# The tanh of a feed-forward block, moved one attention cycle later, with ScalarE in the program's own order

## The chip, the cores and the metric

The kernel runs on one core of a Trainium2 chip. The metric is the device time of one execution in microseconds (us); lower is better. Before the change three runs gave 1499.8, 1505.9 and 1506.9 us, a median of 1505.9 us. A core has five engines with a queue each: TensorE (PE, matrix products), VectorE (DVE), ScalarE (ACT, here exp and tanh), GpSimd (POOL) and SyncE (SP, which here only issues DMAs). Each works through its own list of instructions, and instructions wait for one another through semaphores.

## The reference

One sequence of 2048 tokens of width 512, float32:

```
h  = x + softmax(q k^T / 4) v @ wo       q = LN(x) @ wq (32 heads of 16), one k and one v for all heads
h2 = h + (gelu(LN(h) @ w_gate) * (LN(h) @ w_up)) @ w_down      w_gate, w_up: 512 x 1792
gelu(g) = 0.5 g (1 + tanh(0.798 (g + 0.0447 g^3)))
```

The two halves are an attention block and a gated feed-forward network (FFN). Every float32 product is made of three products of split halves (high and low parts), so most tensors come in pairs such as `gh`/`gl` or `x2h`/`x2l`.

## The kernel before

The sequence is cut in four blocks of 512 queries. Within a block the attention runs over 8 groups of 4 heads, and in a group over 16 chunks of 128 keys. The unit of the attention is a *score*: two matmuls into one PSUM tile `s` of 128 x 1024 (line 283) and one exp of it on ACT into `p` (line 287). Two scores make one chunk, and each chunk then needs its products with V, `weigh` (line 291), which accumulate in the PSUM tile `acc`. After a group `evacuate` copies `acc` out (`oT`, line 300), sends it through DRAM, and after every second group DVE takes four reciprocals (line 321), multiplies and splits the result into `o_hi` and `o_lo`.

PE is shared. While the attention of block b+1 runs, the FFN of block b (with the output projection before it) is woven in, as the Python generator `dense`. The main loop (after line 660) goes in *cycles*: each has 5 or 6 scores, between them a fixed number of FFN matmuls (`shares`, such as 0, 5, 4, 3, 0), and at its end the products with V of the chunks whose exps are old enough (`finish`). Six cycles make a group. Only two `s` tiles exist in this stage, so the third score of a cycle can't start before the first exp of the cycle is done, and during the products with V there is no score for ACT to work on. The FFN of the last block has no attention to be woven into; it is the tail, from about 1355 us on.

In the FFN, `up(f)` (f from 0 to 13, columns of 128) makes the products `pg` and `pu` in two halves, in two successive cycles (`duo`, line 412). Between the halves a one-column copy on DVE (`mark`, line 420) stands as a wait: the second half swaps the array's halves and starts only behind it. When the second half is through, `up` emits on DVE `g` (a copy of `pg`, line 518), `g*g` (520) and one fused step (521) that leave tanh's argument in `ga`; on ACT the tanh (524); and on DVE again two steps on `ga` (525, 526; the latter reads `pu`) and the split into `gh` and `gl` (lines 104, 105). `down` multiplies `gh`/`gl` with w_down for the four f of one run and adds the product to `h` (546); it is emitted one or two `up`s after the run has ended. PSUM holds three one-bank tiles for all FFN products of the main stage (`width = 3`).

What sets the order of the work: an engine named in `tc.manual_schedule` issues its instructions as the Python code emits them. For the others the framework's planner makes the order when the program is built: it plays the program through with estimated durations, and an engine takes what is ready first, the earlier emitted of two that are both ready. Before the change PE and POOL are manual all through, ACT and DVE in the prologue (`prologue` within `with order`), SP in the first stage (up to about 355 us). So in the main stage ACT's order of exps and tanhs, DVE's order and the order of the DMAs on SP are the planner's. What the order says is then kept on the chip: an instruction that waits holds up all behind it on its engine.

At the start, after `prologue`, `first_q` issues three DMAs on ACT's queue (lines 267 and 271) that wait for the bound `m`; and `rest`, emitted after it, has ACT copy the last two blocks of keys out of PSUM (`leave_k`, lines 841 and 843), which POOL (849), PE (857) and DVE (862, 863) then work on. The first scores need the PSUM banks of this stage.

Of the kernel before, what the change touches and what calls it, by code (L numbers as in the profile page):

```python
# [13 lines left out]
AF = mybir.ActivationFunctionType  # L14
ALU = mybir.AluOpType
# [6 lines left out]
GELU_A = 0.044715  # L22
GELU_C = 0.7978845608028654
# [13 lines left out]
def kernel(  # L37
# [12 lines left out]
    nc = tc.nc  # L50
# [49 lines left out]
    def split(eng_hi, hi, lo, src, eng_lo=None):  # L100
        if eng_hi is nc.scalar:
            nc.scalar.activation(hi, src, AF.Copy)
        else:
            eng_hi.tensor_copy(hi, src)  # L104
        (eng_lo or nc.vector).tensor_tensor(lo, src, hi.bitcast(F32), op=ALU.subtract)  # L105
# [19 lines left out]

    def attend(first):
        with ExitStack() as outer:
            with tc.manual_schedule(engines={mybir.EngineType.PE, mybir.EngineType.Pool}):
                run(outer, first)


    def run(outer, first):
# [3 lines left out]
        def set_banks(name):  # L136
            nonlocal ps
            banks.close()
            ps = banks.enter_context(tc.tile_pool(name=name, bufs=1, space=PSUM))
# [92 lines left out]
        if first:  # L232
            set_banks("ps_pro")
            width = 8
            order = tc.manual_schedule(
                engines={mybir.EngineType.Activation, mybir.EngineType.DVE}
            )
            with order:
                rest = prologue(
                    psum1, xT, wq_hi, wq_lo, sel, k2m, project_q(0, nc.scalar),  # L240
                    advance, eb
                )
# [46 lines left out]
        def weigh(acc, p, kc):  # L289
            for j in range(4):  # L290
                nc.tensor.matmul(  # L291
                    acc[32 * j : 32 * j + 32, :], v_sb[:, kc, :], p[:, j, :],
                    start=(kc == 0), stop=(kc == KC - 1), skip_group_check=True,
                )
# [3 lines left out]
        def evacuate(b, g, acc):  # L298
            oT = sb.tile([P, T], F32, tag="oT", bufs=2, name=f"oT_{b}_{g}")
            nc.vector.tensor_copy(oT, acc)  # L300
            nc.sync.dma_start(acc_d[:, g % 4, :], oT)
            c, k = divmod(g, 2)
            if k == 0:
                pair[0] = sb.tile([P, 2, T], F32, tag="oc", bufs=2, name=f"oc_{b}_{c}")
            oc = pair[0]
            view = acc_d[:, g % 4, :].rearrange("(j s e) t -> j e s t", s=2, e=DH)
            for j in range(4):
                r0 = 64 * k + DH * j
                nc.sync.dma_start(oc[r0 : r0 + DH, :, :], view[j])
            if k == 0:  # L310
                return
            if c == 0:
                o_blk[b] = [
                    sb.tile([P, DC, T], F32R, tag=f"o_{w}", bufs=1, name=f"o_{w}_{b}")
                    for w in ("hi", "lo")
                ]
            hi, lo = o_blk[b]

            for t in range(TB):
                sl = slice(t * P, (t + 1) * P)  # L320
                nc.vector.reciprocal(oc[:, 1, sl], oc[:, 1, sl])  # L321
            nc.vector.tensor_tensor(oc[:, 0, :], oc[:, 0, :], oc[:, 1, :], op=ALU.mult)
            split(nc.vector, hi[:, c, :], lo[:, c, :], oc[:, 0, :])
# [110 lines left out]
        def dense(b, tail=False):  # L434
# [71 lines left out]
            def up(f, gh, gl):  # L506
                hi, lo = w1.pop(f)
                terms = [
                    [
                        (wt[:, k, c, :], xt[:, c, :])  # L510
                        for c in range(DC)
                        for wt, xt in ((hi, xT_hi), (hi, xT_lo), (lo, xT_hi))
                    ]
                    for k in range(2)
                ]
                pg, pu = yield from product([f"pg_{b}_{f}", f"pu_{b}_{f}"], terms)
                g = db.tile([P, T], F32, tag="g", bufs=2, name=f"g_{b}_{f}")
                nc.vector.tensor_copy(g, pg)  # L518
                a = db.tile([P, T], F32, tag="ga", bufs=2, name=f"ga_{b}_{f}")
                nc.vector.tensor_tensor(a, g, g, op=ALU.mult)  # L520
                nc.vector.scalar_tensor_tensor(  # L521
                    a, a, 1.0 / GELU_A, g, op0=ALU.add, op1=ALU.mult
                )
                nc.scalar.activation(a, a, AF.Tanh, scale=GELU_A * GELU_C)  # L524
                nc.vector.scalar_tensor_tensor(a, a, 1.0, g, op0=ALU.add, op1=ALU.mult)  # L525
                nc.vector.tensor_tensor(a, a, pu, op=ALU.mult)
                split(nc.vector, gh[:, f % 2, :], gl[:, f % 2, :], a)
                yield CUT

            def down(fs, gs, last):  # L530
# [54 lines left out]
        def finish(n):  # L585
            for _ in range(min(n, len(pend))):
                pb, pg, pkc, pp, pacc, _ = pend.pop(0)
                weigh(pacc, pp, pkc)
                if pkc == KC - 1:
                    evacuate(pb, pg, pacc)  # L590

        def drain():
            nonlocal work
            for _ in work or ():
                pass
            work = None
# [3 lines left out]
        def score(n):  # L600

            nonlocal acc
            i, u = divmod(n, 2)
            b, r = divmod(i, PER)
            g, kc = divmod(r, KC)
            if u == 0:
                if kc == 0:
                    cur["qg"] = qgs.pop((b, g))
                    acc = pss.tile([P, T], F32, tag="acc", bufs=1, name=f"acc_{b}_{g}")
                if kc == 2 and b * NG + g + 1 < NB * NG:  # L610
                    key = divmod(b * NG + g + 1, NG)
                    qgs[key] = load_q(*key)
                cur["p"] = sb.tile([P, 4, T], F32, tag="p", bufs=PB, name=f"p_{i}")
            scores(i, cur["p"], cur["qg"], kc, u)
            if u == 1:
                pend.append((b, g, kc, cur["p"], acc, n))
# [56 lines left out]
        for c in range(LEAD[0], (NB - 1) * NG * len(SIZES)):  # L673
            b, cb = divmod(c, NG * len(SIZES))
            cg = cb % len(SIZES)
            size, kind = SIZES[cg], None
            if b > 0 and cb == LEAD[b]:
                assert work is None
                work, todo = dense(b), list(kinds)
            if work is not None:  # L680
                kind = todo.pop(0)
            if kind == "long":
                shares = LAST if cg == len(SIZES) - 1 else LONG[size]
            elif kind == "short":
                shares = SHORT[size]
            else:
                shares = PLAIN[size]
            due, said = 0, None
            for share in shares:
                score(n)  # L690
                n += 1
                if kind in (None, "gap"):
                    finish(sum(e[5] < n - 1 for e in pend))
                due += share
                while due > 0:
                    said = next(work)
                    if said > 0:
                        due -= 1
                    elif said == CUT:
                        break  # L700

            while work is not None and kind is not None and said not in (CUT, GAP):
                said = next(work)
                assert said < 0, said
            if work is not None and not todo:
                assert next(work, None) is None
                work = None
            finish(sum(e[5] < n - 1 for e in pend) if cg < len(SIZES) - 1 else len(pend))
        drain()
        banks.close()  # L710
# [234 lines left out]
    def exact_maxima():  # L945
        with ExitStack() as gen:
            sb = gen.enter_context(tc.tile_pool(name="gen", bufs=1))
            ps = gen.enter_context(tc.tile_pool(name="gen_ps", bufs=1, space=PSUM))
            with tc.For_i(0, H, 1) as h:
# [18 lines left out]
                for k in range(2):  # L968
# [4 lines left out]
                    )  # L973

    attend(True)

    safe = nc.values_load(flag[0:1, 0:1], min_val=0, max_val=1)
    with tc.If(safe == 0):
        exact_maxima()
        attend(False)  # L980
# [32 lines left out]
```

## Time and profile before

| what | value |
|---|---|
| median of three runs | 1505.9 us (1499.8 to 1506.9) |
| profiled execution, its own time | 1510.7 us |
| its span, first to last instruction | 1508.9 us |
| PE busy | 1428.4 us, 95% |
| ACT busy | 1040.2 us, 69% |
| DVE busy | 530.1 us, 35% |
| main stage (attention with the FFN woven in) | about 355 to 1355 us |
| tail | about 1355 to 1508.9 us |

How to read it: a row of groups has line, engine, operation, tiles and count, then busy time and mean duration in ns, then the engine's idle time ahead of the group and what ended most of it. A row of the timeline has start and duration in us, and in brackets the idle time before it and what released it. The chain that ended last, followed back from the end, runs over PE for 58% of the span. PE's ends are modelled, so that 95% busy still leaves room for waits between its instructions.

### The profile page before, as it was taken

The numbers are of one execution on the slowest core, as the hardware profiler recorded it, in microseconds if no ns is written. First come the engines' busy times: TensorE is split into PE (matmuls) and PEld (weight loads), VectorE is DVE, ScalarE is ACT, GpSimd is POOL, SyncE is SP. The second block draws the span as 40 slices with busy tenths as digits, with TensorE's granted clock in tenths as the row PEclk, the third lists the DMA queues.
The fourth block names the chain that finished last, engine by engine and source line by source line (L and its number), as shares of the span: only waits on it lengthen the run. The fifth ranks groups of instructions, "written<-read, shape, count | busy, mean of one in ns | idle before, by whom it ended". The sixth has DMA issues, their size and how long they took to land.

```text
span 1508.9 us, 24762 instructions
## 1 busy us (share of the span) xinstructions
PE 1428.4 (95%) x10412; PEld 756.3 (50%) x10412; DVE 530.1 (35%) x915; ACT 1040.2 (69%) x1139; POOL 161.7 (11%) x211
## 2 busy tenths in 40 slices
PE   6899999889999999999999999999999999997998
PEld 4533333224445455455455555554455555555886
DVE  7412221203342431423342332423352332425665
ACT  6499999787777777776677777777677777770000
POOL 5424445430000000000000000000000000000000
PEclk9899999989999999999999999999999999999999
DMA  4425666764122323213222422232232323232552
GB/s 159 150 78 189 224 221 212 224 205 137 56 85 78 137 81 109 94 66 129 67 98 66 137 82 107 97 99 95 68 109 78 113 82 129 72 105 74 194 193 86
DMA packets 76109, 180.53 MB, mean 120 GB/s; under 512 B 8506, under 2 KB 22842, under 8 KB 68790
## 3 DMA queue, kind: packets, MB, share of 16 engines
q1 hardware_dynamic: 75870, 178.81, 35.5%
q8 instruction: 83, 1.36, 0.4%
q14 instruction: 36, 0.29, 0.1%
q10 hardware_dynamic: 120, 0.07, 0.0%
HBM read 131.13 MB, written 47.71 MB: 119 GB/s over the span
## 4 chain that ended last, share of the span: by engine, by line
PE 58%; ACT 13%; DVE 8%; DMA 8%; issue 6%; POOL 5%; SPq 2%; DVEq 0%; POOLq 0%; ACTq 0%
PE acc L291 22%; ACT p L287 12%; PE s L283 11%; PE pu L412 5%; PE pd L412 4%; DMA w_1r<-in_B_w_up_dram 3%; PE pg L429 3%; PE pg L412 3%; PE pd L429 3%; PE pu L429 3%; DVE oc L321 2%; DMA acc_d<-oT 2%; PE pp L412 1%; POOL w_1b L105 1%; PE pq L170 1%
## 5 line engine op out<-in xcount | busy, mean ns | idle before, releaser
L287 ACT ACTIVATE p<-s 128x1024 f32<-128x1024 f32 x1024 | 970.7, 1031 | 261.5 <-PE s L283 260.6
L291 PE MATMUL acc<-p,v_sb 128*32 128x512 f32 x4096 | 496.9, 604 | 2.0 <-DVE oT L300 2.0
L283 PE MATMUL s<-qg,kaug 50*128 50x512 f32 x1984 | 394.1, 436 | 35.3 <-ACT p L287 31.1
L283 PEld LDWEIGHTS s<-qg,kaug 50*128 50x128 f32 x1984 | 172.1, 185 | 320.9 <-ACT p L287 207.6
L291 PEld LDWEIGHTS acc<-p,v_sb 128*32 128x32 f32 x4096 | 112.9, 110 | 252.1 <-issue 243.3
L412 PE MATMUL pu<-x2h,w 64*128 64x512 f32 x672 | 233.6, 394 | 2.4 <-DVE mark_pu L420 0.9
L412 PE MATMUL pg<-x2h,w 64*128 64x512 f32 x672 | 233.5, 394 | 0.8 <-DVE x2h L104 0.8
L412 PEld LDWEIGHTS pu<-x2h,w 64*128 64x128 f32 x672 | 125.1, 186 | 17.8 <-DVE mark_pu L420 3.6
L412 PE MATMUL pg<-x2l,w 64*128 64x512 f32 x336 | 132.1, 393 | 0.1
L412 PE MATMUL pu<-x2l,w 64*128 64x512 f32 x336 | 132.0, 393 | 0.0
L412 PEld LDWEIGHTS pg<-x2h,w 64*128 64x128 f32 x672 | 125.1, 186 | 12.9 <-DVE x2h L104 2.0
L524 ACT ACTIVATE ga<-ga 128x512 f32<-128x512 f32 x56 | 35.3, 631 | 135.6 <-DVE ga L521 135.6
L518 DVE COPY g<-pg 128x512 f32<-128x512 f32 x56 | 38.7, 691 | 232.7 <-PE pg L412 224.5
L113 POOL TENSOR_SCALAR rstd<-mv 128x1 f32<-128x1 f32 x16 | 3.5, 219 | 1041.4 <-DVE mv L111 1041.4
L412 PE MATMUL pd<-w,gh 64*128 64x512 f32 x672 | 105.4, 391 | 0.3 <-DVE mark_pd L420 0.3
L546 DVE TENSOR_TENSOR h<-h,pd 128x512 f32<-128x512 f32 x64 | 41.9, 684 | 138.3 <-PE pd L412 117.3
L321 DVE RECIPROCAL oc<-oc 128x128 f32<-128x128 f32 x64 | 54.1, 907 | 55.9 <-DMA oc<-acc_d 53.9
L412 PEld LDWEIGHTS pd<-w,gh 64*128 64x128 f32 x672 | 63.4, 185 | 15.5 <-issue 0.8
L412 PEld LDWEIGHTS pg<-x2l,w 64*128 64x128 f32 x336 | 62.6, 186 | 8.4 <-DVE x2l L105 1.1
L412 PE MATMUL pd<-w,gl 64*128 64x512 f32 x336 | 66.4, 392 | 0.0
L412 PEld LDWEIGHTS pu<-x2l,w 64*128 64x128 f32 x336 | 62.6, 186 | 6.8
L525 DVE SCALAR_TENSOR_TENSOR ga<-ga,g 128x512 f32<-128x512 f32 x56 | 38.8, 692 | 39.1 <-ACT ga L524 39.1
(176 smaller groups left out, 1219.6 us busy)
## 6 DMA issues: line engine op xcount, KB each, us to landing
w<-w_d SPq DMA_DIRECT2D x84, 1024.0 KB
qg<-q_d SPq DMA_DIRECT2D x62, 200.0 KB
q_d<-qh SPq DMA_DIRECT2D x32, 256.0 KB
acc_d<-oT SPq DMA_DIRECT2D x32, 256.0 KB
oc<-acc_d SPq DMA_DIRECT2D x128, 64.0 KB
w_d<-w_0b SPq DMA_DIRECT2D x14, 512.0 KB
w_d<-w_1b SPq DMA_DIRECT2D x14, 512.0 KB
x<-in_A_x_dram SPq DMA_DIRECT2D x16, 256.0 KB
```

The source lines that it names most:

```text
L105: (eng_lo or nc.vector).tensor_tensor(lo, src, hi.bitcast(F32), op=ALU.subtract)
L170: nc.tensor.matmul(pq, wt[:, d, c * P : (c + 1) * P], xt[:, d, :], start=(n == 0), stop=(n == 3 * DC - 1),)
L283: nc.tensor.matmul(s[:, a, :], kaug[rows, kc * P : (kc + 1) * P], qg[rows, u, :], start=True, stop=True,)
L287: nc.scalar.activation(p[:, 2 * u : 2 * u + 2, :], s, AF.Exp, scale=SCALE)
L291: nc.tensor.matmul(acc[32 * j : 32 * j + 32, :], v_sb[:, kc, :], p[:, j, :], start=(kc == 0), stop=(kc == KC - 1), skip_group_check=True,)
L321: nc.vector.reciprocal(oc[:, 1, sl], oc[:, 1, sl])
L412: nc.tensor.matmul(banks[k], lhsT[rows], rhs[rows], start=(turn == 0 and i == 0), stop=(turn == 1 and i == n - 1), skip_group_check=True,)
L429: nc.tensor.matmul(bank, lhsT, rhs, start=(i == 0), stop=(i == len(ts) - 1))
L518: nc.vector.tensor_copy(g, pg)
L524: nc.scalar.activation(a, a, AF.Tanh, scale=GELU_A * GELU_C)
L525: nc.vector.scalar_tensor_tensor(a, a, 1.0, g, op0=ALU.add, op1=ALU.mult)
L546: nc.vector.tensor_tensor(hs[t], hs[t], pd, op=ALU.add)
```

## The change

ACT is added to the manual engines for the whole of `attend`, so its order is that in which the code emits (the separate mention in the prologue goes, as it is implied). In `up`, the tanh and the four DVE steps behind it (two on `ga`, the split into `gh` and `gl`) are no longer emitted at once but put into a function, `gate`, on a list `gates`. The main loop takes the list at the start of a cycle, and emits what was on it near the end of that cycle: after the cycle's scores and FFN matmuls, ahead of its products with V. So a tanh whose `up` ended in cycle c is emitted at the end of cycle c+1, behind that cycle's exps. In the tail each gate is emitted at once, as before.

```diff
-            with tc.manual_schedule(engines={mybir.EngineType.PE, mybir.EngineType.Pool}):
+            with tc.manual_schedule(
+                engines={mybir.EngineType.PE, mybir.EngineType.Pool, mybir.EngineType.Activation}
+            ):
                 run(outer, first)
...
-            order = tc.manual_schedule(
-                engines={mybir.EngineType.Activation, mybir.EngineType.DVE}
-            )
+            order = tc.manual_schedule(engines={mybir.EngineType.DVE})
...
-                nc.scalar.activation(a, a, AF.Tanh, scale=GELU_A * GELU_C)
-                nc.vector.scalar_tensor_tensor(a, a, 1.0, g, op0=ALU.add, op1=ALU.mult)
-                nc.vector.tensor_tensor(a, a, pu, op=ALU.mult)
-                split(nc.vector, gh[:, f % 2, :], gl[:, f % 2, :], a)
+
+                def gate():
+                    nc.scalar.activation(a, a, AF.Tanh, scale=GELU_A * GELU_C)
+                    nc.vector.scalar_tensor_tensor(a, a, 1.0, g, op0=ALU.add, op1=ALU.mult)
+                    nc.vector.tensor_tensor(a, a, pu, op=ALU.mult)
+                    split(nc.vector, gh[:, f % 2, :], gl[:, f % 2, :], a)
+
+                gates.append(gate)
+                if tail:
+                    open_gates()
                 yield CUT
...
+        gates = []
+
+        def open_gates():
+            while gates:
+                gates.pop(0)()
...
             due, said = 0, None
+            ready, gates[:] = gates[:], []
             for share in shares:
                 score(n)
...
                 said = next(work)
                 assert said < 0, said
+            for gate in ready:
+                gate()
             if work is not None and not todo:
```

## The prediction

> **What bounds the kernel now.** I read the page first, then the list of waits, then ACT's and DVE's timelines around the tanhs, then stretches of one cycle each. The page and the waits:
>
> ```profile
> PE 1428.4 (95%) x10412; PEld 756.3 (50%) x10412; DVE 530.1 (35%) x915; ACT 1040.2 (69%) x1139; POOL 161.7 (11%) x211
> ...
> PE 58%; ACT 13%; DVE 8%; DMA 8%; issue 6%; POOL 5%; SPq 2%; DVEq 0%; POOLq 0%; ACTq 0%
> ...
> L287 ACT ACTIVATE p<-s 128x1024 f32<-128x1024 f32 x1024 | 970.7, 1031 | 261.5 <-PE s L283 260.6
> L524 ACT ACTIVATE ga<-ga 128x512 f32<-128x512 f32 x56 | 35.3, 631 | 135.6 <-DVE ga L521 135.6
> ```
>
> ```profile
> ACT ga L524 <- DVE ga L521: 135.6, 56, 15.7
> ...
> PEld pu L412 <- DVE mark_pu L420: 3.6, 6, 0.6
> ...
> PEld s L283 <- ACT ga L524: 3.4, 4, 0.8
> ```
>
> PE is the bound; ACT has 31% to spare. The 135.6 us that ACT sits before tanhs look like the prize, and are not: 14 of the 56 are in the tail (4.8 us each, two of 15.7) where PE never waits for them, and most of the 42 others fall into the products with V, where ACT has no score anyway. Only 3.4 us of PE's waits are put down to a tanh directly. What a late tanh costs must be read from the length of cycles. First ACT and then DVE around the worst one:
>
> ```profile
> 428.93 4.80 ACT L287 ACTIVATE p<-s 128x1024 f32<-128x1024 f32 x5 [1.10 <-PE s L283]
> 438.96 0.63 ACT L524 ACTIVATE ga<-ga 128x512 f32<-128x512 f32 x1 [5.22 <-DVE ga L521]
> 439.49 2.83 ACT L287 ACTIVATE p<-s 128x1024 f32<-128x1024 f32 x3
> ```
>
> ```profile
> 431.82 3.39 DVE L321 RECIPROCAL oc<-oc 128x128 f32<-128x128 f32 x4 [5.73 <-DMA oc<-acc_d]
> 435.24 0.69 DVE L322 TENSOR_TENSOR oc<-oc 128x512 f32<-128x512 f32 x1
> 435.97 0.43 DVE L104 CAST o_hi<-oc 128x512 fp32r<-128x512 f32 x1
> 436.31 0.68 DVE L518 COPY g<-pg 128x512 f32<-128x512 f32 x1
> ```
>
> DVE stood before the reciprocals for a DMA, so the copy of `pg` queued behind them, and the tanh, came late; the next cycle's first exp stood behind the tanh although its score (435.25) was there. Now cycles, in each of which I take start to start (columns: length, then busy time by engine, then PE's granted clock, DMA):
>
> ```profile
> 435.25:446.48 11.23, 8.31 (x55) 4.64 (x52) 6.26 (x11) 5.42 (x6) 0.00 (x0) 0.85 0.11 46
> 481.90:487.89 5.99, 5.99 (x54) 3.46 (x51) 0.16 (x1) 4.78 (x5) 0.00 (x0) 1.00 0.00 0
> 523.33:531.38 8.05, 6.29 (x55) 3.47 (x51) 4.64 (x9) 5.31 (x6) 0.00 (x0) 1.00 0.16 67
> 608.22:616.87 8.65, 6.56 (x56) 3.57 (x52) 5.26 (x10) 5.29 (x6) 0.00 (x0) 1.00 0.15 61
> 951.54:957.97 6.43, 6.25 (x55) 3.46 (x52) 2.73 (x6) 4.91 (x5) 0.00 (x0) 1.00 0.12 24
> ...
> 957.97:965.66 7.69, 7.54 (x64) 3.80 (x60) 2.83 (x6) 6.12 (x7) 0.00 (x0) 1.00 0.29 118
> 916.10:923.67 7.57, 7.40 (x64) 3.79 (x60) 0.16 (x1) 5.61 (x6) 0.00 (x0) 1.00 0.47 182
> ```
>
> Rows one, three, four and five have the shape of row two (5 scores, 16 instructions of products with V), which takes 6.0 us undisturbed. So three cycles of the first block lose 5.2, 2.05 and 2.65 us, 9.9 in all. Six cycles of the second and third block are like row five: 0.43 each, 2.6 together. Eight are like 957.97 (6 scores, 7.69 against 7.57): 0.12 each. All others keep the length of their shape. What can be won is therefore about 13 us of 1510.7, not 135.6.
>
> **The change, part by part.** The sum is against the profiled execution's 1510.7 us; the median, 1505.9, is 0.9968 of it, and I scale by that at the end.
>
> *The tanh itself.* 42 tanhs of 0.63 us move behind the exps of the next cycle. There ACT waits 1.1 us (cycles with 16 instructions of V) to 2.05 us (with 24) for the next score, and tanh's argument has been ready for a whole cycle. Cost nothing, hidden in that wait; without it, 42 x 0.63 = 26 us. What was behind a late tanh is free: the next first exp no longer waits for DVE.
>
> *The eight cycles at 7.69.* Their first exp starts 0.24 us late (0.10 in others), behind a tanh. Gain 8 x 0.12 = 0.9; bounds 0 and 0.9.
>
> *The three late cycles.* The tanh's wait goes, but `g` is still copied late, and `pu` of the next `up` needs the bank that this copy frees: in the cycle at 435.25 PE got it at 437.05 instead of 435.8. And now the gate of the `up` before (0.69 + 0.69 + 0.43 + 0.69 = 2.5 us of DVE) falls into the same cycle as the reciprocals. In its favour, `oT` loses a 0.69 us step ahead of it, so that reciprocals come 0.6 us earlier. At 435: the gate's tanh would end at 428.5, its DVE steps at 431.0, inside the wait for the DMA; `g` is out at about 436.3, or 437.4 with half of the gate behind the reciprocals, or 438.8 with all of it: a stall of 0.6, 1.6 or 3.0. I take 1.4, and 0.7 for the clock (below): gain 3.1, bounds 0.5 and 4.6. At 523: tanh out at 516.5, gate until 519.0, then 3.4 + 0.7 + 0.4 and `g` 0.7 give 524.3 to 525.1 where PE wants the bank at 523.9: stall 0.8, gain 1.2, bounds 0.9 and 1.65. At 608 the same counting gives 0 to 1.1; stall 0.5, gain 2.1, bounds 1.5 and 2.65. Sum 6.4, bounds 2.9 and 8.9.
>
> *The clock.* The cycle at 435.25 has granted clock 0.85: 3.4 us of it, 441.0 to 444.4, ran at 0.50, after 436 to 441 in which PE was busy for 2.08 of 5.0 us. The cycle at 523.33, with a wait of 1.76 us, kept 1.00. My 0.7 is some half of the 1.7 us which 3.4 us at half clock cost, since the stall left is nearer to the second row. [...]
>
> *The six marks.* At 946 to 952 DVE did reciprocals, then gate steps between the other steps, and `mark_pu` last, 0.43 too late for PE. The gate's `gh` and `gl` (0.43 + 0.69 = 1.1 us) leave that spot, and nothing is in front of the reciprocals but their DMA. Against it: the gate of the cycle before can hold `oT` up by 1.0 us. Bare of other work, `oT` to reciprocal took 6.4 us (1357.90 to 1364.32) against 8.4 here (938.03 to 946.41), so there are 2 us of room. Gain 2.6; bounds -2.5 (marks 0.4 later still) and 2.6.
>
> *The start.* ACT's four copies of `leave_k` (2.1 us, at 51.7 to 54.4) go behind the three ACT-issued DMAs, which wait for `m`, and so run when these are out (61.7 by the trace). Then PE's transposes (0.6) and DVE's copies (0.3) end near 64.9, where the first score now starts at 64.38: 0.5 late, or 2.0 if DVE's 1.5 us `qs` gets in between. But the last square for the bound, now at 52.73 behind two of those copies, comes 0.9 us earlier, and with it `m`, the DMAs and all that follows. I take 0, bounds -2.0 and 0.9. POOL's six steps (8.8 us from 58.1) end some 2 us later, in front of 8 us of idle time before its next work at 76.7. No DMA is moved on SP by the code, and no instruction is added anywhere.
>
> *Held longer.* `pu` stays in PSUM for one cycle more. With three banks: the next `up` takes the free one and that of `pg`, as before; the held one is wanted only a cycle after its gate. Cost nothing; that cover is a cycle of 6 to 7.5 us.
>
> *The tail.* Gates open at once, ACT's order there is already that of the code: 0.
>
> Sum: 0.9 + 6.4 + 2.6 + 0 = 9.9; 1510.7 - 9.9 = 1500.8, times 0.9968 = 1496.0 us. Own range: all best ends give 13.3 (1492.6), all worst ends -1.6 (1507.5).
>
> **The rivals.**
>
> *The bank takes the place of the tanh.* DVE stays as late as its DMA, PE waits for `g` instead of ACT for `ga`: the three cycles gain 2.9, the marks 0, the start costs 0.8: 0.9 + 2.9 - 0.8 = 3.0, so 1502.9. For it: 1.3 us of PE's wait for `g` at 437.05 are there already. Against: two of three times `g` was in time before.
>
> *The DMAs change places.* SP's order is the planner's, and it re-plans. One block end lost 4.0 us (a cycle of 10.04 from 694.13, against 6.00), as the store of `oT` took 7.87 us beside a weight load. If two more ends come to that, 3.0 - 8.0 = -5.0: 1510.9, still within what counts as no change. Against: the other ends show none.
>
> *Slower: the gate in front of the mark.* DVE serves in its planned order. If the planner puts a gate ahead of the `mark` of the same cycle, PE's next half waits for tanh and gate. From the last exp's end: 0.63 + 2.5 + 0.16 = 3.3 us, where PE wants the mark 1.1 (16 V) to 2.05 us (24 V) after it: 1.2 to 2.2, say 1.7 each. In a third of the 42: 14 x 1.7 = 24, less the 3 gained: 1527. It decides from the second gate step on; one alone (0.63 + 0.69 + 0.16 = 1.5) costs at most 0.4. Against: marks end about 1.2 us ahead of the tanh's new place (935.29 against an exp that ends at 935.82, plus 0.63), and are emitted before it.
>
> **How the numbers follow.** Faster or slower counts from 0.5% (7.5 us; the three runs before span 7.1). Forecast 0.48 (faster); bank 0.23 and DMAs 0.10 (both within); gate before mark 0.19 (slower). Faster 0.48, same 0.33, slower 0.19. The range leaves out the slower rival alone: from 1488 (the best end less the spread of runs) to 1514 (the second rival and 3 us of that spread).
>
> **What would show it.** Every tanh of the main stage 0 to 0.2 us behind an exp, ACT's wait for `ga` down from 135.6 to the tail's 90 or so; the cycles after the late reciprocals at 6.0 to 7.5 us, with PE waiting for `g` (L518); no wait for `mark_pu` of 0.6. Wrong would be: waits for `mark` in many cycles, `g` later by the whole gate, the first exp after 66, or long cycles at block ends.

## The result, and the profile after

The changed kernel took 1493.97 us (median of four runs, 1492.66 to 1495.33) against 1505.01 us before (four runs, 1499.8 to 1506.9). The ratio is 0.9932 with a 95% interval of 0.9904 to 0.9960: faster by 0.7%, where 1496.0 us had been forecast. Run again later on another occasion the change took 1494.36 us, at a ratio of 0.9926 (0.9898 to 0.9955).

The profiled execution after took 1492.66 us with a span of 1490.9 us, 18.0 us less than the profiled span before. That is more than the change is worth; the experiments show below where the rest belongs. The page after, first the engines and the chain, then two groups:

```profile
PE 1419.6 (95%) x10412; PEld 755.2 (51%) x10412; DVE 530.4 (36%) x915; ACT 1036.6 (70%) x1139; POOL 160.9 (11%) x211
...
PE 64%; ACT 15%; DMA 6%; issue 5%; POOL 5%; DVE 2%; SPq 1%; ACTq 0%; POOLq 0%; DVEq 0%
...
L287 ACT ACTIVATE p<-s 128x1024 f32<-128x1024 f32 x1024 | 970.8, 1031 | 282.2 <-PE s L283 281.5
...
L526 ACT ACTIVATE ga<-ga 128x512 f32<-128x512 f32 x56 | 36.2, 646 | 91.4 <-DVE ga L521 91.4
```

The 42 tanhs of the main stage no longer wait for DVE: 135.6 us have become 91.4, over 14 waits, which are the tail's. The 44 us that went were mostly idle time that ACT has at the end of a cycle in any case, and ACT's wait for scores grew from 261.5 to 282.2 us. So the gain has to be read from cycles again. The three that were late (before 11.23, 8.05 and 8.65 us), then one of the six with a late mark (6.43) and one of the eight at 7.69; columns as in the table of cycles before:

```profile
430.38:436.77 6.39, 6.39 (x54) 3.73 (x50) 2.98 (x7) 5.43 (x6) 0.00 (x0) 1.00 0.19 79
513.66:520.05 6.39, 6.39 (x55) 3.73 (x52) 2.98 (x7) 5.43 (x6) 0.00 (x0) 1.00 0.21 86
596.92:603.31 6.39, 6.39 (x55) 3.66 (x51) 2.98 (x7) 5.42 (x6) 0.00 (x0) 1.00 0.20 82
934.66:940.65 5.99, 5.99 (x54) 3.47 (x50) 3.46 (x6) 4.79 (x5) 0.00 (x0) 1.00 0.11 26
940.65:948.22 7.57, 7.42 (x65) 3.81 (x61) 1.12 (x4) 6.11 (x7) 0.00 (x0) 1.00 0.29 120
```

The late ones lose 0.39 each now, the marks and the eight nothing. Two rows of the list of waits in the main stage, of PE's weight loads:

```profile
PEld s L283 <- ACT ga L526: 15.1, 18, 0.8
...
PEld pu L412 <- DVE g L518: 1.0, 3, 0.3
```

The tanh is named for 15.1 us where it was 3.4, but all cycles other than the three late ones and the one at the first block's end have the undisturbed length of their shape: a row of this list is no cost by itself. The three waits for `g` are in the three late cycles. DVE and ACT around the first of them, in their timelines:

```profile
425.41 0.69 DVE L105 TENSOR_TENSOR gl<-ga,gh 128x512 fp32r<-128x512 f32 x1
426.02 3.38 DVE L321 RECIPROCAL oc<-oc 128x128 f32<-128x128 f32 x4
...
430.50 0.68 DVE L518 COPY g<-pg 128x512 f32<-128x512 f32 x1
```

```profile
430.92 3.04 ACT L287 ACTIVATE p<-s 128x1024 f32<-128x1024 f32 x3 [2.06 <-PE s L283]
434.16 1.94 ACT L287 ACTIVATE p<-s 128x1024 f32<-128x1024 f32 x2 [0.19 <-PE s L283]
435.98 0.63 ACT L526 ACTIVATE ga<-ga 128x512 f32<-128x512 f32 x1
```

The copy of `pg` still comes behind the reciprocals, at 430.50 in a cycle that starts at 430.38. These begin right behind the last step of the gate, with no idle time between, so that it is now the gate and not the DMA that sets when they start. But the exps begin at 430.92 in spite of it, and the tanh stands behind the fifth, where ACT would wait for the products with V.

Split by stages (start of a given score's exp in the two profiles), the 18.0 us are: 4.9 up to the start of the main stage, 8.6 in the first block's cycles, 2.2 in the first cycle after them (10.04 against 7.86), 3.5 in the second and third block, and 1.1 lost again in the tail.

### The profile page after: what moved, and what is told of

Read it like the earlier page. It is cut to its first block, busy times and chain, and to the rows that moved or that the text cites. A ratio compares the mean times of both kernels' runs of the same rounds, so it can differ in the third digit from the quotient of the medians.

```text
span 1490.9 us, 24774 instructions
## 1 busy us (share of the span) xinstructions
PE 1419.6 (95%) x10412; PEld 755.2 (51%) x10412; DVE 530.4 (36%) x915; ACT 1036.6 (70%) x1139; POOL 160.9 (11%) x211
## 4 chain that ended last, share of the span: by engine, by line
PE 64%; ACT 15%; DMA 6%; issue 5%; POOL 5%; DVE 2%; SPq 1%; ACTq 0%; POOLq 0%; DVEq 0%
PE acc L291 26%; ACT p L287 14%; PE s L283 13%; PE pu L412 5%; PE pd L412 4%; PE pg L412 4%; DMA w_1r<-in_B_w_up_dram 3%; PE pg L429 3%; PE pd L429 3%; PE pu L429 3%; DMA acc_d<-oT 2%; PE pp L412 1%; PE pq L172 1%; POOL w_1b L105 1%; PE pp L429 1%
## 5 line engine op out<-in xcount | busy, mean ns | idle before, releaser
L287 ACT ACTIVATE p<-s 128x1024 f32<-128x1024 f32 x1024 | 970.8, 1031 | 282.2 <-PE s L283 281.5
L526 ACT ACTIVATE ga<-ga 128x512 f32<-128x512 f32 x56 | 36.2, 646 | 91.4 <-DVE ga L521 91.4
```

The source lines that it names most:

```text
L287: nc.scalar.activation(p[:, 2 * u : 2 * u + 2, :], s, AF.Exp, scale=SCALE)
```

## The experiments

The theory: two gains in the main stage, the tanh taken from in front of the next cycle's exps (late cycles, and the eight), and the DVE steps taken from in front of the marks. The lists of instructions for PE, POOL and SP come out the same before and after; so what else differs between the two profiles, outside ACT's and DVE's order, should be scatter.

### The order alone

```diff
-                if tail:
-                    open_gates()
+                open_gates()
```

> ACT manual as in the change, but each gate opened at once, so that tanh and the four DVE steps are emitted where they were before. Theory (the gain is the later place of the tanh and of the steps behind it): the three late cycles of the first block stay at 11.2, 8.0 and 8.6 us and the six marks at 6.4; time as before, 1503 to 1507 us, ratio 0.998 to 1.002. Rival (ACT in the code's order is in itself what helps): 1492 to 1497 us.

Measured: 1504.6 us, ratio 0.9998 (0.9980 to 1.0017). The late cycles, one of the marks and one of the eight:

```profile
429.15:437.92 8.77, 6.69 (x55) 3.65 (x52) 5.37 (x10) 5.30 (x6) 0.00 (x0) 1.00 0.14 57
514.79:522.57 7.78, 6.26 (x54) 3.47 (x51) 4.40 (x8) 5.30 (x6) 0.00 (x0) 1.00 0.16 66
599.43:608.98 9.55, 7.83 (x54) 4.58 (x51) 4.61 (x9) 5.42 (x6) 0.00 (x0) 0.82 0.13 56
939.90:946.35 6.45, 6.27 (x56) 3.46 (x52) 2.73 (x6) 4.91 (x5) 0.00 (x0) 1.00 0.16 25
946.35:954.03 7.68, 7.54 (x65) 3.82 (x61) 2.83 (x6) 6.12 (x7) 0.00 (x0) 1.00 0.28 117
```

All losses are back, the three late ones in other sizes than expected (11.2, 8.0 and 8.6). With the gates opened at once the code's order of ACT is the planner's but for one place: the four copies at the start, which come behind the DMAs as in the change. So the run shows that the manual order by itself brings nothing, and it is one more execution of the main stage with ACT's order of before.

### The gate alone

```diff
-            with tc.manual_schedule(
-                engines={mybir.EngineType.PE, mybir.EngineType.Pool, mybir.EngineType.Activation}
-            ):
+            with tc.manual_schedule(engines={mybir.EngineType.PE, mybir.EngineType.Pool}):
```

and the prologue's `{Activation, DVE}` as before.

> The gates as in the change, but ACT left to the planner in the main stage. The planner takes what is ready first, and a tanh is ready long before the place where the code emits it; its list for every engine comes out as that of the kernel before. Theory: so the time is that of before, 1503 to 1507 us, and the profile shows by how much the first stage (to the first score past 355 us) and the cycle at the end of the first block vary between runs of one and the same order: I expect the 4.9 us of the first stage and the 2.2 us of the block end, which the profile after has over the profile before, to be such scatter. Rival (the deferral works without the manual order): 1492 to 1497 us.

Measured: 1504.02 us, ratio 0.9989 (0.9968 to 1.0010). The late cycles were 11.34, 11.07 and 7.37 us. The lists of ACT and DVE are those of before, instruction for instruction: the planner, left to itself, undoes the deferral. So neither half of the change does anything without the other that these intervals of 0.2% could show.

As a second profile of the order of before it also shows the scatter. The exp of score 272 (start of the main stage) began at 354.7 us before and at 346.1 here; in all profiles, with either order, at 346.1 to 354.7 (after: 349.8 and, again, 354.0). The cycle at the first block's end took 10.04 before (3.4 us of it at half clock), 7.82 here, 7.86 and 8.11 after. The 4.9 and the 2.2 us are therefore no part of the change.

### The tanh in the middle of the cycle

```diff
-            for share in shares:
+            for place, share in enumerate(shares):
                 score(n)
                 n += 1
+                if place == 2:
+                    for gate in ready:
+                        gate()
...
-            for gate in ready:
-                gate()
```

> As the change, but the gate is emitted behind the third score of the next cycle and not at its end, so the tanh stands between exps. Theory (the tanh is free only in the wait for the products with V): later exps of the cycle start up to 0.63 us later, PE's last scores wait for them; 42 cycles by 0.2 to 0.63 make 8 to 26 us over the change, 1502 to 1520 us. Rival (ACT is busy for 70% and has room anywhere): 1492 to 1497 us.

Measured: 1501.83 us, ratio 0.9964 (0.9944 to 0.9983), above the change by 7.5 to 7.9 us in medians of different occasions, by 5 to 6 in ratios, and by 6.8 in the lengths of the cycles. Cycles: one with a gate and 6 scores (6.74 in the change), a late one, one after a mark, and another with 6 scores (7.57 in the change):

```profile
420.23:427.47 7.24, 6.60 (x56) 3.58 (x52) 3.26 (x6) 6.11 (x7) 0.00 (x0) 1.00 0.55 200
434.40:440.41 6.01, 6.01 (x54) 3.46 (x50) 3.70 (x7) 5.20 (x6) 0.00 (x0) 1.00 0.21 87
941.67:947.66 5.99, 5.99 (x54) 3.47 (x51) 2.26 (x4) 4.78 (x5) 0.00 (x0) 1.00 0.17 27
947.66:955.74 8.08, 7.41 (x64) 3.80 (x61) 2.74 (x6) 6.12 (x7) 0.00 (x0) 1.00 0.27 112
```

Fourteen such cycles with 6 scores grow by 0.5 us each (7 us); those with 5 scores hardly at all, save two marks (6.76 and 6.25). The time came out just under what the theory said (1502 to 1520 us), since it had charged all 42. ACT has room in a cycle of 5 scores and none in one of 6. The three late cycles are even free of loss (6.0): with the gate earlier the reciprocals begin 5.3 to 6.1 us ahead of the cycle, as soon as their DMA lets them, where the change mostly has 4.4. The price is paid two cycles ahead, in three of the fourteen.

### The DVE steps alone

```diff
+                nc.scalar.activation(a, a, AF.Tanh, scale=GELU_A * GELU_C)
+                one = db.tile([P, 1], F32, tag="one", bufs=2, name=f"one_{b}_{f}")
                 def gate():
-                    nc.scalar.activation(a, a, AF.Tanh, scale=GELU_A * GELU_C)
-                    nc.vector.scalar_tensor_tensor(a, a, 1.0, g, op0=ALU.add, op1=ALU.mult)
+                    nc.scalar.activation(one, power[:, 1:2], AF.Copy, scale=2.0)
+                    nc.vector.scalar_tensor_tensor(a, a, one, g, op0=ALU.add, op1=ALU.mult)
```

> Tanh emitted at once as before; only the four DVE steps move a cycle on, as their first takes its constant 1 from a one-column tile that ACT writes (0.2 us) where the gate opens. Theory (two separate gains): the six marks are in time (2.5 us gained), the three late cycles and the eight at 7.69 stay (9.7 us not gained), so 1501 to 1505 us, with ACT's waits for tanh's argument at 130 us or more. Rival (the DVE steps, not the tanh, held up the cycles): 1492 to 1497 us, late cycles gone.

Measured: 1504.18 us, ratio 0.9982 (0.9961 to 1.0003); ACT waits 135.0 us for tanh's argument. The late cycles, one after a mark, one of the eight:

```profile
431.21:439.79 8.58, 6.50 (x54) 3.61 (x50) 3.24 (x7) 5.40 (x7) 0.00 (x0) 1.00 0.15 62
516.66:527.15 10.49, 8.32 (x55) 4.35 (x51) 4.14 (x8) 5.51 (x7) 0.00 (x0) 0.84 0.13 52
604.01:613.83 9.82, 7.74 (x54) 4.62 (x50) 3.08 (x6) 5.59 (x7) 0.00 (x0) 0.83 0.13 54
944.63:950.63 6.00, 6.00 (x54) 3.46 (x51) 3.11 (x6) 4.78 (x5) 0.00 (x0) 1.00 0.18 26
950.63:958.31 7.68, 7.53 (x65) 3.83 (x62) 1.54 (x4) 6.20 (x8) 0.00 (x0) 1.00 0.28 117
```

All six marks are in time (5.99 to 6.01), the three and the eight stay late. In the whole time the 2.5 us can't be told from nothing (the interval reaches 1.0003), in the cycles they can. The copy of `pg` starts here within 0.32 us of the start of the late cycle, as in the change (0.12), so the tanh's place alone makes 2.2 to 4.1 us a cycle, two of them with a drop of the clock. The two gains are separate, each with the cause that was named.

### The mark behind the gate

```diff
-                    mark = sb.tile([P, 1], F32, tag="mark", bufs=2, name=f"mark_{names[1]}")
-                    nc.vector.tensor_copy(mark, banks[1][:, :1])
                     yield CUT
+                    mark = sb.tile([P, 1], F32, tag="mark", bufs=2, name=f"mark_{names[1]}")
+                    if behind:
+                        nc.vector.tensor_tensor(
+                            mark, banks[1][:, :1], behind.pop(), op=ALU.add
+                        )
+                    else:
+                        nc.vector.tensor_copy(mark, banks[1][:, :1])
```

with `behind[:] = [gl[:, f % 2, :1].bitcast(F32)]` at the end of `gate`.

> The change, and each mark that follows an open gate reads one column of that gate's gl, so that DVE does the four gate steps ahead of the mark: the order that the slower rival of the prediction spoke of. Theory (the order of mark and gate decides the sign): PE's second halves wait 1.2 us (cycles with 24 instructions of V) to 2.2 us (16) for some 42 marks, 50 to 90 us over the change, 1545 to 1585 us, and waits for mark in the list. Rival (PE has other work in front and hides it): below 1505 us.

Measured, a single run: 1563.53 us. Two rows of the list of waits, of PE:

```profile
PE pu L412 <- DVE mark_pu L422: 44.9, 33, 2.2
...
PE pd L412 <- DVE mark_pd L422: 12.0, 9, 2.4
```

42 waits, 56.9 us. The slower rival's mechanism is real: forced on all 42 gates (the rival had a third of them) it costs 69 us over the change, close to 42 times its 1.7 us, 71. Of the 12 us beyond the waits some 10 are, by estimate, half of the six stretches of 3.41 us at half clock that this run has in its main stage and the change hasn't. In the change the planner puts each mark first: each of the 42 gates begins on DVE 0.07 to 2.6 us after the start of a mark, so the rival has no place.

### Three tanhs where one stood

```diff
                 def gate():
+                    for more in range(0 if tail else 2):
+                        nc.scalar.activation(
+                            gh[:, f % 2, :], a, AF.Tanh, scale=GELU_A * GELU_C
+                        )
                     nc.scalar.activation(a, a, AF.Tanh, scale=GELU_A * GELU_C)
```

> The change with two more tanhs of the same size in each gate of the main stage (into gh, which is overwritten later): 1.9 us of ACT where 0.63 stood. Theory (free as long as it fits the wait of 1.1 to 1.3 us at 16 and 2.0 us at 24 instructions of V): the ten gates of the first block that fall in front of a short wait delay the next first exp by 0.3 to 0.6 us and their next cycles grow by 0.2 to 0.5; the 32 others cost nothing; 2 to 5 us over the change, 1496 to 1499 us. Rival (ACT's time counts wherever it stands): 42 x 1.26 = 53 us more, 1547 us.

Measured: 1497.2 us, ratio 0.9950 (0.9932 to 0.9968), 2.8 us above the change. Two cycles that follow a gate before a short wait (6.91 and 7.57 in the change), and one after a gate before a long one:

```profile
426.49:434.04 7.55, 7.15 (x62) 3.72 (x59) 6.12 (x9) 5.91 (x8) 0.00 (x0) 1.00 0.31 93
440.35:448.33 7.98, 7.63 (x66) 3.81 (x62) 4.58 (x7) 6.57 (x8) 0.00 (x0) 1.00 0.28 89
940.69:946.71 6.02, 6.02 (x54) 3.47 (x50) 4.41 (x7) 5.09 (x6) 0.00 (x0) 1.00 0.16 29
```

Ten cycles of the first block grow by 0.4 to 0.64 us, none of the others by more than 0.2. The ten make 5.3 us; some fifty others are 0.05 to 0.08 us shorter, 3.0 us together, and why is open. 42 x 1.26 = 53 us more of ACT cost 3. So a tanh of 0.63 is free where the change puts it.

### The copies of the keys early

```diff
+            for b in range(NB - 2, NB):
+                vTs[b] = leave_k(b, pks[b])
+
             def rest():
                 low_k(1, vTs[1])
                 for b in range(NB - 2, NB):
-                    vTs[b] = leave_k(b, pks[b])
                     low_k(b, vTs[b])
```

> The change, and ACT's four copies of the last two key blocks emitted at the end of the prologue, ahead of the three ACT-issued DMAs and still behind the last square for the bound. Theory (the copies behind the DMAs hold up PE's transposes and so the first score, which cancels what the earlier bound brings): first exp at 62 to 63 us instead of 65.0, whole time 1 to 2.5 us less than the change, 1490 to 1494 us. Rival (the first score waits for DVE or the DMA of q anyway): first exp at 64 to 65, time as the change.

Measured: 1493.35 us, ratio 0.9917 (0.9891 to 0.9944), beside the change run again on the same chip. First the change's ACT at the start, then this kernel's:

```profile
58.27 1.22 ACTq L267 DMA_DIRECT2D qg_first<-m  x2
...
61.94 0.61 ACT L860 ACTIVATE vT<-pk 128x512 f32<-128x512 f32 x1
65.03 2.85 ACT L287 ACTIVATE p<-s 128x1024 f32<-128x1024 f32 x3 [2.48 <-PE s L283]
```

```profile
53.32 0.57 ACT L860 ACTIVATE vT<-pk 128x512 f32<-128x512 f32 x1
58.23 1.22 ACTq L267 DMA_DIRECT2D qg_first<-m  x2
...
62.40 3.77 ACT L287 ACTIVATE p<-s 128x1024 f32<-128x1024 f32 x4 [8.50 <-PE s L283]
```

The first exp comes 2.6 us earlier. The seven profiles with the change's start have it at 64.2 to 65.2 us; the second profile of the order of before has 62.41. The 65.00 of the first profile before were an accident: there a `qh` on ACT waited 3.60 us for a DMA, 2.09 in the other, and later a `qs` on DVE took 1.78 us, 0.68 in the other; the two make the 2.6 us. In the whole time the 2.6 us can't be told from scatter (1.0 us between medians, intervals overlapping); this is the lowest median of all kernels here, no more.

### The change again

> The change itself again, for a narrower interval and a second profile. Theory: 1492 to 1496 us, ratio 0.992 to 0.995; in the profile the three cycles at 6.4 us, the six at 6.0, the eight at 7.57 again, while the start of the main stage (exp 272, 349.8 in the first profile) and the cycle at the first block's end (7.86) may move by some us. Rival (part of the 18 us between the two first profiles comes from the first stage for good): main stage begins at 349 to 351 again and the ratio is 0.990 or lower.

Measured: 1494.36 us, ratio 0.9926 (0.9898 to 0.9955). The late cycles were 6.46, 6.39 and 6.85, marks and the eight as in the first profile, the main stage began at 354.0 and not at 349.8: scatter, as expected.

## Why the prediction was right, point by point

**What bounds the kernel.** Right: of the 135.6 us of ACT's waits 44 went, and the time fell by 11.

**The tanh itself, 0.** Right, with the reason given: three tanhs cost 3 us in place of 53, and one in the middle of a cycle costs 0.5 where the cycle has 6 scores.

**The eight cycles, 0.9, and the six marks, 2.6.** Right in place and size: 7.57 and 6.0 after. The second and third block, which hold little else, gained 3.5 us together. That the marks owe it to the DVE steps, and the eight to the tanh, is shown by the steps moved alone.

**The three late cycles, 6.4.** Right in mechanism, too small. Over four profiles with the tanh in its old place they lose 9.9, 8.1, 11.8 and 10.9 us, 10.2 on average; over three with the change's, 1.2, 1.7 and 2.2, or 1.7. The gain is about 8.5. The stall over PE's bank that I charged with 1.4, 0.8 and 0.5 us, and 0.7 for the clock, was 0.39 in six of nine cycles and 1.4 at most. It was the first of the three cases weighed there (0.6): the whole gate of the `up` before ran in front of the reciprocals (its last step at 425.41, they at 426.02 above), so that `g` came 0.3 us late and not 1 to 2. These 0.39 us are the gate's own cost, which holds the reciprocals up; with the gate earlier, in the middle of the cycle, they are gone. In the cycles of 6.85 and 7.38 DVE stood another 0.41 and 0.90 us behind the gate for the DMA.

**The clock.** No drop of the granted clock in the main stage of any of the three profiles with the change's order there (the change twice, and the kernel with the early copies); in the first of them the granted clock is 1.00 from 349.8 to 1341.0 us. I had taken half a drop, 0.7 us, for the first cycle, an estimate from the two cycles at 435.25 and 523.33; none came.

**The start, 0.** This step failed. The copies behind the DMAs delay the first exp by 1.8 to 2.8 us, about my bad bound of 2.0; what I set against it, 0.9 us from an earlier square, does not exist. In a start without the slow DMA the square is at 51.2 us in either order, since it waits for its product (1.27 us in the profile after), not for the copies. I had taken a delay from the one profile that had a late `qh`.

**The tail, and `pu` held longer, 0.** No wait of PE for the gate's read of `pu` appears in the list after. The tail's 1.1 us go with its own half-clock stretches (6.8 us more at half in that profile); it has the same order, and in the second profile of the change they are not there.

By the measured terms, with 2.3 for the start: 8.5 + 2.6 + 0.9 - 2.3 = 9.7 us, without it 12.0, against 11.0 and 10.6 measured. The forecast's 9.9 was the right sum from a term 2.1 too small and one up to 2.3 too good; that the two cancel is luck. Whether the start's delay reaches the end in full is open: it is smaller than the first stage's scatter, and the order alone, which has the later start and else ACT's order of before, shows no loss (ratio 0.9998) in an interval that would hide it (up to 1.0017).

**The rivals.** The bank did not take the tanh's place: 0.39 us a time. The DMAs kept their order on SP. The gate was not put in front of the mark; made to be, it costs about what its 1.7 us a gate make.

**The range.** Its lower edge of 1488 us does not follow from its own words: the best end, 1492.6, less the runs' spread of 7.1 is 1485.5. Nothing here hangs on it.

## What to carry to other kernels

An engine's waits in the list say who waited, not what it cost: here 44 us of them went for a gain of 11, and the price stood only in the length of the cycles, compared with undisturbed cycles of the same shape. Work on a side engine was nearly free where that engine waits for the bound one anyway (53 us more of ACT cost 3), and dear ahead of what the bound engine needs next (the late cycles with the tanh in its old place are 2.2 to 4.1 us longer in the steps alone); so a step with a whole cycle to spare belongs behind the last instruction that is urgent, and with an order written down, since a planner that takes what is ready puts it back (1504.02 us in the gate alone). When a whole engine's order is fixed by hand, look at every place where its order changes: at the start, of which the change did not speak, the first exp came some 2 us later.

## What the runs showed of the hardware

The granted clock fell to 0.50 for 3.4 us after some PE waits of about 2 us and less, and after others it did not. Single waits of 2.09 us (cycle at 608.22 before) and 2.08 (at 429.15 with the order alone) had no drop behind them; one of 1.72, at 601.33 with the order alone, had one, from 603.41 to 606.81, and so had 0.83 and 2.09 within 4.3 us in the cycle at 435.25 before, from 441.01 to 444.43. The price can be read: late cycles with the tanh in its old place took 7.4 to 8.8 us without a drop, and 9.6 to 11.3 with one.

The stretches of 3.41 us that end at three of the drops, columns as in the table of cycles: before, the order alone, and the steps alone:

```profile
437.60:441.01 3.41, 1.32 (x11) 0.79 (x9) 2.65 (x4) 2.05 (x3) 0.00 (x0) 1.00 0.00 0
599.99:603.41 3.42, 1.70 (x16) 1.07 (x14) 2.66 (x5) 1.96 (x3) 0.00 (x0) 1.00 0.21 86
519.04:522.46 3.42, 1.34 (x11) 1.08 (x12) 0.56 (x1) 2.83 (x4) 0.00 (x0) 1.00 0.02 5
```

PE was busy in them for 1.32, 1.70 and 1.34 us. Before, it was busy for 1.32 of the 3.41 us up to the end of the wait at 612.48 too, and the granted clock stayed at 1.00. And one and the same wait of 2.08 us had no drop behind it in the steps alone where it ended at 435.39, and a drop where it ended at 521.23. So neither the length of a single wait nor PE's busy time up to its end tells the two kinds apart; what does is left open. In the late cycles of the profile after PE was busy for 6.39 of 6.39 us, at a granted clock of 1.00.

In the first stage, two executions with the same lists of instructions on all five engines (before, and the gate alone) differed by 8.6 us (the start of score 272's exp, 354.7 and 346.1), the earlier with 10.2 us at half clock up to there and the later with 27.3; this is as much as most of the effects studied here; two profiles alone would have put 7 us of scatter down to the change.
